# Reordering the opening of a fused Fourier-mixing and SiLU kernel: products summed on TensorE, roundings placed elsewhere, other queues for the last rows

## The chip, the cores and the metric

The kernel runs on one core of a Trainium2 chip. The metric is the device time of one execution in microseconds (us); the time before is 2628.63 us, the median of three runs (2626.27 to 2629.31). The five engines of the core work side by side and wait for each other through semaphores: TensorE (PE, its weight loads are PEld), VectorE (DVE), ScalarE (ACT), GpSimd (POOL) and SyncE (SP). SP, ACT and POOL also issue the DMA transfers; each of them does so in its own program order, so a transfer that has to wait holds up everything behind it on the engine that issues it.

## The reference

Two stages, one after the other. The first is a filter in the frequency domain along the sequence, for 8 batches of 3008 positions and 256 channels; the second is a two-layer network with SiLU on each of the 24064 tokens, with 2048 hidden features.

```python
X = np.fft.rfft(x, axis=1)                    # x: (8, 3008, 256)
F = (filt_r + 1j * filt_i)[None, :, :]        # (1505, 256)
y = np.fft.irfft(X * F, n=x.shape[1], axis=1).astype(np.float32)

t = y.reshape(8 * 3008, 256)
h = t @ w_in                                  # (256, 2048)
g = h * (1.0 / (1.0 + np.exp(-h)))
out = (g @ w_out).astype(np.float32)          # (2048, 256)
```

The weights arrive as float64 words and are made into float32 on the chip (below: a rounding).

## The kernel before

The network runs as a long loop in which TensorE is kept full; the Fourier stage of batch b+1 is spread over the loop that works on batch b. Only batch 0 has nothing to hide behind: its Fourier stage, with the loads and the roundings of the first weights, is the opening, and the loop starts when it is done. The change touches the opening alone. Its stages, in order:

1. Loads of the input, the filter, tables and raw weights. `stage1_first(k)`, k = 0 to 15: two products into one PSUM bank each, then a VectorE transpose out of the bank.
2. For each of six groups g: `forward(g)` (TensorE), `multiply(g, k)` for the two banks k (VectorE: the bank times the real and times the imaginary filter, giving z and p), `add(g, k)` (the complex product from z and p), `inverse_first(g)` (TensorE, then two ScalarE copies and two stores to DRAM).
3. `load_t4(g)` for g = 0 to 3: the stored rows come back, transposed by the addressing. Rows 0 to 39 are those of groups 0 to 4, rows 40 to 47 those of group 5. They are loaded in two parts.
4. `stage3(g)` for g = 0 to 3: TensorE, and a copy of each bank into y by VectorE or ScalarE. With y the loop can begin.

Between these the roundings `rounded(j, ...)` of weights 0 to 8 are run, on VectorE and ScalarE in turn.

```python
def multiply(g, k):
    z = zpool.tile([128, 2, C], FP32, name=f"z_{b}_{g}_{k}", tag="z")      # 4 buffers
    pt = ppool.tile([128, 2, C], FP32, name=f"p_{b}_{g}_{k}", tag="p")     # 2 buffers
    for m, dst in ((0, z), (1, pt)):
        nc.vector.tensor_tensor(out=dst, in0=banks[g][k],
                                in1=f_t[m][:, g, k:k + 1, :].to_broadcast([128, 2, C]), op=ALU.mult)
    prods[g].append((z, pt))

def add(g, k):
    z, pt = prods[g][k]
    eng = nc.vector if b > 0 or (g == NG - 1 and k == 0) else nc.gpsimd
    eng.tensor_tensor(out=z[:, 0], in0=z[:, 0], in1=pt[:, 1], op=ALU.subtract)
    eng.tensor_tensor(out=z[:, 1], in0=z[:, 1], in1=pt[:, 0], op=ALU.add)

def inverse_first(g):
    ps = [bank(b, f"pc_{b}_{g}_{i}") for i in range(2)]
    zs = [z for z, _ in prods.pop(g)]
    for h in range(2):
        table = e_t[:, g] if h == 0 else minus[g // 4][:, g % 4]
        for ri in range(2):
            for i in range(2):
                rows = slice(64 * i, 64 * i + 64)
                for k in range(2):
                    nc.tensor.matmul(out=ps[i][64 * k:64 * k + 64, h, :], lhsT=table[rows, k, ri, :],
                                     rhs=zs[k][rows, ri, :], ...)             # 16 products
    for i, pool, tag in ((0, qpool, "q"), (1, opool, "o")):
        qt = pool.tile([128, 2, C], FP32, name=f"q_{b}_{g}_{i}", tag=tag)
        nc.scalar.copy(out=qt, in_=ps[i])
        a0 = 8 * g + 4 * i
        queue = nc.sync if g == NG - 1 and i == 0 else nc.scalar
        queue.dma_start(out=d2[a0:a0 + 4]..., in_=qt)

def load_t4(g, first=0, last=2 * NS):
    ...                                        # groups 2 and 3 take buffers of the pool "t"
    for h in range(2):
        queue = nc.scalar if first > 0 and h == 1 else nc.sync
        queue.dma_start(out=t4s[g][64 * h + first:64 * h + last],
                        in_=d2[first:last, 4 * g:4 * g + 4, h, :])
```

`bank` gives batch 0 the six PSUM banks in turn, two for each call of `forward`, `inverse_first` and `stage3`. A rounding of two weights is, in order: on VectorE two bit operations for each weight; on ScalarE two activations for each and two more for the even one; on VectorE two multiply-adds, a clamp and two merges; then `place_weights` (two products for each weight) and, behind an odd weight, `combine_weights` (four sums).

The order of the opening:

```python
weights(0, 1)                                  # weights(...): loads of raw words, on SP
place = part["load_first"]()
rounded(0, 1, part=0)
...                                            # loads of filter, tables, weights 2 to 8; table "minus"
for k in range(16):
    part["stage1_first"](k)
rounded(0, 1, part=1)
for g in range(NG):
    part["forward"](g)
    for k in range(2):
        part["multiply"](g, k)
    for k in range(2):
        part["add"](g, k)
    if g > 0:
        part["inverse_first"](g - 1)
    if g in (1, 3):
        rounded(g + 1, g + 2)
for g in range(4):
    part["load_t4"](g, 0, 40)
part["inverse_first"](NG - 1)
for g in range(4):
    part["load_t4"](g, 40, 2 * NS)
for u in range(2):
    second["load_x"](u)
rounded(6, 7)
rounded(8)
for g in range(4):
    part["stage3"](g)
weights(9, 10, 11, 12, 13)
```

Of the kernel before, what the change touches and what calls it, by code (L numbers as in the profile page):

```python
# [46 lines left out]
FP32 = mybir.dt.float32  # L47
U32 = mybir.dt.uint32
AFT = mybir.ActivationFunctionType
# [4 lines left out]
B, S, C = 8, 3008, 256  # L54
DFF = 2048
N1, N2 = 47, 64
NS, NG = 24, 6
# [110 lines left out]
def kernel(  # L168
# [9 lines left out]
    nc = tc.nc  # L178
# [14 lines left out]
    cpool = pool("consts", 1)  # L193
# [4 lines left out]
    tpool = pool("t12", 2)  # L198
    ppool = pool("p", 2)
# [4 lines left out]
    abcpool = pool("abc", 2)  # L204
# [14 lines left out]

    w_t = cpool.tile([128, NJP, 7, 2, 128], FP32)  # L220
    warm = cpool.tile([128, 1], FP32)
    bias_t = cpool.tile([128, 4], FP32)
    x_all = xpool.tile([128, 2, 2, 2 * C], FP32)
    x_t = [x_all[:, i] for i in range(2)]

# [37 lines left out]
    def spectral(b):  # L263
# [171 lines left out]

        def multiply(g, k):
            z = zpool.tile([128, 2, C], FP32, name=f"z_{b}_{g}_{k}", tag="z")
            pt = ppool.tile([128, 2, C], FP32, name=f"p_{b}_{g}_{k}", tag="p")
            for m, dst in ((0, z), (1, pt)):
                nc.vector.tensor_tensor(  # L440
                    out=dst, in0=banks[g][k],
                    in1=f_t[m][:, g, k:k + 1, :].to_broadcast([128, 2, C]), op=ALU.mult)
            prods[g].append((z, pt))

        def add(g, k):
            z, pt = prods[g][k]
            eng = nc.vector if b > 0 or (g == NG - 1 and k == 0) else nc.gpsimd
            eng.tensor_tensor(out=z[:, 0], in0=z[:, 0], in1=pt[:, 1], op=ALU.subtract)
            eng.tensor_tensor(out=z[:, 1], in0=z[:, 1], in1=pt[:, 0], op=ALU.add)

# [13 lines left out]
                                             skip_group_check=True)  # L464
            halves[g] = ps, []

        def inverse_first(g):

            ps = [bank(b, f"pc_{b}_{g}_{i}") for i in range(2)]
            zs = [z for z, _ in prods.pop(g)]  # L470
            for h in range(2):
                table = e_t[:, g] if h == 0 else minus[g // 4][:, g % 4]
                for ri in range(2):
                    for i in range(2):
                        rows = slice(64 * i, 64 * i + 64)
                        for k in range(2):

                            nc.tensor.matmul(out=ps[i][64 * k:64 * k + 64, h, :], lhsT=table[rows, k, ri, :],  # L478
                                             rhs=zs[k][rows, ri, :], start=(h == 0 and ri == 0),
                                             stop=(ri == 1), skip_group_check=True)  # L480
            for i, pool, tag in ((0, qpool, "q"), (1, opool, "o")):
                qt = pool.tile([128, 2, C], FP32, name=f"q_{b}_{g}_{i}", tag=tag)
                nc.scalar.copy(out=qt, in_=ps[i])
                a0 = 8 * g + 4 * i
                queue = nc.sync if g == NG - 1 and i == 0 else nc.scalar
                queue.dma_start(out=d2[a0:a0 + 4].rearrange("a n h c -> (a n) h c"), in_=qt)

        def even(g, i, n=1):
            qt = qpool.tile([128, 2, 2, C], FP32, name=f"q_{b}_{g}_{i}", tag="q")
# [14 lines left out]
        def load_t4(g, first=0, last=2 * NS):  # L504
            if first == 0 and b == 0 and g in (2, 3):
                t4s[g] = tpool.tile([128, 4, C], FP32, name=f"t4_{b}_{g}", tag="t")
            elif first == 0:
                t4s[g] = t4pool.tile([128, 4, C], FP32, name=f"t4_{b}_{g}", tag="t4")
            for h in range(2):
                queue = nc.scalar if first > 0 and h == 1 else nc.sync  # L510
                queue.dma_start(out=t4s[g][64 * h + first:64 * h + last],
                                in_=d2[first:last, 4 * g:4 * g + 4, h, :])

# [302 lines left out]
    def place_weights(j):  # L816
        mf, ef = raws.pop(j)
        for w in range(2):
            cols = slice(256 * w, 256 * w + 256)
            dst = places(j, w) if w == 0 else places(j, w).rearrange("p k (q i) -> p k q i", q=4)  # L820
            v.tensor_tensor(out=dst, in0=columns(mf[:, cols], w), in1=columns(ef[:, cols], w),
                            op=ALU.mult)
        if j % 2 and not 8 < j < 15:
            combine_weights(j // 2)

    def load_exact(j):
        for k in range(2):
            nc.sync.dma_start(out=places(j, 0)[:, k],
                              in_=moe_w_in[128 * k:128 * k + 128, 128 * j:128 * j + 128])
            nc.sync.dma_start(out=places(j, 1)[:, k].rearrange("p (q i) -> p q i", q=4),  # L830
                              in_=columns(moe_w_out[128 * j:128 * j + 128, :], 1)[:, k])
        if j % 2 and not 8 < j < 15:
            combine_weights(j // 2)

    def combine_weights(jp, part=None):

        def w(c):
            return w_t[:, jp, c]
        if part != 1:
            combine(v, w(S1), w(S3), w(A22), ALU.add)  # L840
            combine(v, w(S2), w(S1), w(A11), ALU.subtract)
        if part != 0:
            combine(v, w(S3), w(A11), w(S3), ALU.subtract)
            combine(v, w(S4), w(A12), w(S2), ALU.subtract)

    def weights(*js):
        for j in js:
            if wide:
                load_weights(j)

    def rounded(*js, part=None):

        if wide and part != 1:
            round_weights(*js)
        for j in js:
            if wide and part != 0:
                place_weights(j)
            if not wide and part != 0:
                load_exact(j)
# [4 lines left out]
    for i, value in enumerate((-896.0, 255.0, 255.0 * (1 << 23))):  # L864
        nc.gpsimd.memset(bias_t[:, i:i + 1], value)
    for j in range(4):
        nc.gpsimd.memset(bias_t[32 * j:32 * j + 32, 3:4], 1.0 if j % 2 == 0 else -1.0)
    part, second = spectral(0), spectral(1)
    weights(0, 1)
    place = part["load_first"]()  # L870
# [9 lines left out]
    weights(*range(4, 9))  # L880

    minus = [typool.tile([128, 4, 2, 2, 64], FP32, name=f"minus_{i}", tag="ty") for i in range(2)]
    for g in range(NG):
        nc.scalar.activation(out=minus[g // 4][:, g % 4], in_=e_t[:, g], func=AFT.Identity,
                             scale=bias_t[:, 3:4])
    for k in range(16):
        part["stage1_first"](k)
    rounded(0, 1, part=1)
    for g in range(NG):
        part["forward"](g)  # L890
        for k in range(2):
            part["multiply"](g, k)
        for k in range(2):
            part["add"](g, k)
        if g > 0:
            part["inverse_first"](g - 1)
        if g in (1, 3):
            rounded(g + 1, g + 2)
    for g in range(4):
        part["load_t4"](g, 0, 40)  # L900
    part["inverse_first"](NG - 1)
    for g in range(4):
        part["load_t4"](g, 40, 2 * NS)
    for u in range(2):
        second["load_x"](u)
    rounded(6, 7)
    rounded(8)
    for g in range(4):
        part["stage3"](g)
    weights(9, 10, 11, 12, 13)  # L910
    early[0] = None
    plan_rest(0, part)
    for g in (4, 5):
# [77 lines left out]
```

## Time and profile before

The span of the profiled execution is 2626.4 us. The times below are from its start; "records" are instructions as the profiler counts them, and a float32 product leaves two.

| stage | from, us | to, us |
|---|---|---|
| first product of `stage1_first` to last transpose | 14.73 | 35.36 |
| first `multiply` (group 0) to last `multiply` (group 5) | 38.11 | 76.95 |
| last product of `inverse_first(5)` | | 80.83 |
| first store of group 5 issued, last one issued | 82.26 | 86.35 |
| last rows of `load_t4` issued | 92.82 | 94.44 |
| `stage3`, four groups | 94.91 | 109.31 |
| first product of the loop | 110.27 | |

The page's first part gives the busy time of each engine over the whole span, its second part the busy tenths in 40 slices; the first two slices are the opening. A row of the timeline has the start, the duration, the engine, the line of the kernel, the operation with its tiles, and in brackets how long the engine was idle before it and what it had waited for. A row of the table by stretches has the length, then for each engine the busy time and the number of records, and at its end the TensorE clock (1.00 is full), the busy share of the DMA engines and what they moved.

### The profile page before, as it was taken

Reading aid. Unit: us, or ns where it says so; the run is one execution under the profiler, and the core shown is the slowest. Engines: PE = TensorE matmul, PEld = TensorE weight load, DVE = VectorE, ACT = ScalarE, POOL = GpSimd, SP = SyncE. Lnnn points to the kernel's source line nnn. Section 1 sums busy time; section 2 is a strip of 40 time slices with the busy share of each in tenths; the row PEclk is TensorE's granted clock in tenths of the full one; section 3 lists DMA queues with packets and bytes.
Section 4 is the critical chain, followed back from the end, with each engine's and each line's share of the span. In section 5 each row is a group of like instructions: output and inputs, shape, how many; then the busy total and the mean of one; then the engine's idle time right before and its main releaser. Section 6 shows DMA issues by size and latency. Waiting matters only on the chain.

```text
span 2626.4 us, 47875 instructions
## 1 busy us (share of the span) xinstructions
PE 2554.7 (97%) x18688; PEld 2173.0 (83%) x18688; DVE 1706.6 (65%) x3590; ACT 1104.3 (42%) x3015; POOL 424.3 (16%) x662
## 2 busy tenths in 40 slices
PE   5599999999999999999999999999999999999998
PEld 3378888888888888888888888888888888888987
DVE  6676766666666666666666666666766666555554
ACT  2354444444444444444444434444344444444443
POOL 1121112111211111111112111221112111100100
PEclk8699999999999999999999999999999999999999
DMA  7432222312332123222222322232122311210000
GB/s 234 140 96 61 65 57 72 85 45 64 79 71 65 45 73 71 63 65 72 66 57 56 81 66 62 63 76 62 65 63 69 82 45 29 56 22 21 9 17 16
DMA packets 200267, 171.05 MB, mean 65 GB/s; under 512 B 122212, under 2 KB 174276, under 8 KB 199252
## 3 DMA queue, kind: packets, MB, share of 16 engines
q1 hardware_dynamic: 178808, 117.46, 18.4%
q0 software_dynamic: 16704, 44.06, 5.4%
q10 hardware_dynamic: 4528, 6.46, 0.8%
q8 instruction: 147, 2.41, 0.4%
q14 instruction: 80, 0.66, 0.1%
HBM read 96.05 MB, written 81.26 MB: 68 GB/s over the span
## 4 chain that ended last, share of the span: by engine, by line
PE 95%; DMA 2%; DVE 1%; ACT 1%; ACTq 0%; POOL 0%; issue 0%; SPq 0%; DVEq 0%; POOLq 0%
PE acc L693 43%; PE px L634 26%; PE pyz L634 19%; PE pd L523 3%; PE pb L428 2%; PE pc L461 2%; PE pf L398 1%; PE pa L326 1%; PE pa L335 0%; DMA w_t<-in_x_dram 0%; PE pc L478 0%; DMA d<-q 0%; DMA filt<-in_filt_r_dram 0%; DMA t<-d 0%; DMA d_t<-d_tbl 0%; DVE w_t L605 0%
## 5 line engine op out<-in xcount | busy, mean ns | idle before, releaser
L693 PE MATMUL acc<-g,w_t 128*128 128x256 f32 (+1 forms) x5376 | 1512.0, 375 | 0.4 <-DVE g L605 0.4
L693 PEld LDWEIGHTS acc<-g,w_t 128*128 128x128 f32 x5376 | 1021.3, 190 | 115.7 <-DVE g L605 0.8
L605 DVE TENSOR_TENSOR g<-pyz,abc 128x256 f32<-128x256 f32 (+1 forms) x1152 | 479.9, 417 | 539.8 <-ACT abc L655 298.6
L605 DVE TENSOR_TENSOR g<-g 128x256 f32<-128x256 f32 (+3 forms) x1152 | 616.9, 535 | 196.8 <-ACT g L638 183.6
L634 PE MATMUL px<-ty,w_t 128*128 128x256 f32 (+1 forms) x2304 | 686.9, 380 | 0.5 <-ACT abc L655 0.5
L638 ACT ACTIVATE g<-g 128x256 f32<-128x256 f32 (+1 forms) x1152 | 472.9, 410 | 245.7 <-DVE g L605 245.7
L605 POOL TENSOR_TENSOR s<-s 128x256 f32<-128x256 f32 (+1 forms) x329 | 259.7, 806 | 1455.0 <-DVE s L711 1404.8
L634 PEld LDWEIGHTS px<-ty,w_t 128*128 128x128 f32 x2304 | 424.0, 190 | 83.3 <-issue 25.3
L634 PE MATMUL pyz<-y,w_t 128*128 128x256 f32 (+1 forms) x1536 | 453.7, 377 | 0.7 <-DVE g L605 0.6
L634 PEld LDWEIGHTS pyz<-y,w_t 128*128 128x128 f32 x1536 | 283.4, 189 | 46.6 <-DVE g L605 5.9
L649 ACT COPY abc<-px 128x256 f32<-128x256 f32 (+1 forms) x384 | 141.5, 368 | 364.4 <-PE px L634 364.4
L638 ACT ACTIVATE g<-px 128x256 f32<-128x256 f32 (+1 forms) x384 | 146.1, 380 | 307.4 <-PE px L634 307.3
L655 ACT COPY abc<-px 128x256 f32<-128x256 f32 (+1 forms) x384 | 144.0, 375 | 309.7 <-PE px L634 309.7
L634 PE MATMUL px<-y,w_t 128*128 128x256 f32 (+1 forms) x768 | 229.8, 381 | 1.0 <-ACT y L246 1.0
L634 PE MATMUL pyz<-ty,w_t 128*128 128x256 f32 (+1 forms) x768 | 225.6, 375 | 0.0
L634 PEld LDWEIGHTS px<-y,w_t 128*128 128x128 f32 x768 | 142.1, 189 | 40.0 <-ACT g L638 15.5
L634 PEld LDWEIGHTS pyz<-ty,w_t 128*128 128x128 f32 x768 | 146.0, 190 | 16.9 <-DVE g L605 0.5
L642 ACT COPY abc<-px 128x256 f32<-128x256 f32 (+1 forms) x384 | 135.3, 352 | 2.7 <-PE px L634 1.3
L244 DVE COPY y<-pd 128x376 f32<-128x376 f32 x64 | 51.2, 806 | 98.2 <-PE pd L523 98.2
L523 PEld LDWEIGHTS pd<-wi_t,t 48*64 48x64 f32 x4096 | 68.9, 140 | 40.7 <-issue 33.8
L523 PE MATMUL pd<-wi_t,t 48*64 48x47 f32 x4096 | 76.6, 239 | 20.7 <-DMA t<-d 14.1
L246 ACT COPY y<-pd 128x376 f32<-128x376 f32 x64 | 51.5, 811 | 90.2 <-PE pd L523 90.2
(83 smaller groups left out, 1305.3 us busy)
## 6 DMA issues: line engine op xcount, KB each, us to landing
t<-d SPq DMA_DIRECT2D x120, 192.0 KB
t<-d SPq DMA_DIRECT2D x84, 256.0 KB
d<-q POOLq DMA_DIRECT2D x84, 256.0 KB, 2.7
out_dram<-o SPq DMA_DIRECT2D x636, 32.0 KB
d<-tf POOLq DMA_DIRECT2D x144, 96.0 KB, 2.4
xr<-in_x_dram SPq DMA_DIRECT2D x6, 1472.0 KB
x_all<-in_x_dram SPq DMA_DIRECT2D x72, 96.0 KB
x_all<-xr SPq DMA_DIRECT2D x72, 96.0 KB
```

The lines of the kernel that those rows point to most:

```text
L244: nc.vector.tensor_copy(out=dst, in_=src)
L246: nc.scalar.copy(out=dst, in_=src)
L428: nc.tensor.matmul(out=ps[k][32 * j:32 * j + 32, ri, :], lhsT=d_t[rows, 4 * g + at, ri, :], rhs=t2[rows, at, :], start=True, stop=True)
L461: nc.tensor.matmul(out=ps[j][64 * k:64 * k + 64, a, :], lhsT=e_t[rows, g + a, k, ri, :], rhs=zs[k][rows, ri, :], start=(a == 0 and ri == 0 ...
L523: nc.tensor.matmul(out=ps[h][c0:c0 + 64, cb, i, :], lhsT=t4s[g][rows, i, 128 * cb + c0:128 * cb + c0 + 64], rhs=wi_t[rows, :], start=True, ...
L605: eng.tensor_tensor(out=out, in0=in0, in1=in1, op=op)
L634: nc.tensor.matmul(out=out, lhsT=w_t[:, jp, c, 0], rhs=rhs, start=start, stop=True, skip_group_check=True)
L638: nc.scalar.activation(out=g[:, k, 0:n], in_=g[:, k, 0:n] if src is None else src, func=AFT.Silu)
L642: nc.scalar.copy(out=sums[:, 0, 0:n], in_=xo)
L649: nc.scalar.copy(out=sums[:, 1, 0:n], in_=xo)
L655: nc.scalar.copy(out=sums[:, 2, 0:n], in_=xo)
L693: nc.tensor.matmul(out=acc[pair][i][:, h, 0:n], lhsT=w_t[:, jp, c, 1], rhs=g[:, k, 0:n], start=(jp == 0 and h == 0), stop=last, skip_group ...
```

## The change

It has five parts, all ahead of the loop.

- **Products summed in the inverse.** For groups 1, 4 and 5 no `add` is run. `inverse_first` takes z and p as they are and adds up four terms in PSUM in place of two: 32 products in place of 16. For the signs it needs two tables, `neg`, made by ScalarE once and kept in the two buffers of the pool "t". One half of the p tiles moves to the pool "abc", so that four are there at a time. The adds of groups 0, 2 and 3 stay on GpSimd.
- **Roundings ahead of the copies.** Weights 2 and 3 are rounded behind `multiply(1)` as before, but stand ahead of the ScalarE copies of group 0; weights 4 and 5 behind `multiply(4)` in place of `multiply(3)`; weights 6 and 7 ahead of `inverse_first(5)` in place of behind the last `load_t4`. The combination of weights 0 and 1 goes behind `multiply(0)`.
- **Other queues.** The half of t4's last rows that ScalarE issued is issued by GpSimd; the store of group 5 that SP issued is issued by ScalarE.
- **Early loads.** The two first loads of batch 1 (`load_x`) and the raw weights 9 to 12 are issued in the middle of the groups, weight 13 behind the roundings.
- **Idle products.** 22 products of the table wx with itself, 128 columns each, whose result nobody reads, run on TensorE from the arrival of that table on, ahead of `stage1_first`.

```diff
@@ multiply, add
-            pt = ppool.tile([128, 2, C], FP32, name=f"p_{b}_{g}_{k}", tag="p")
+            if b == 0 and k == 1:
+                pt = abcpool.tile([128, 3, C], FP32, name=f"p_{b}_{g}_{k}", tag="abc")[:, 0:2]
+            else:
+                pt = ppool.tile([128, 2, C], FP32, name=f"p_{b}_{g}_{k}", tag="p")
-            eng = nc.vector if b > 0 or (g == NG - 1 and k == 0) else nc.gpsimd
+            eng = nc.vector if b > 0 else nc.gpsimd
@@ inverse_first
-        def inverse_first(g):
+        def inverse_first(g, added):
-            zs = [z for z, _ in prods.pop(g)]
+            pairs = prods.pop(g)
                 table = e_t[:, g] if h == 0 else minus[g // 4][:, g % 4]
-                for ri in range(2):
+                terms = [(table[:, :, 0], 0, 0), (table[:, :, 1], 0, 1)]
+                if not added:
+                    terms += [(table[:, :, 1], 1, 0), (neg[h][:, g], 1, 1)]
+                for t, (lhs, which, ri) in enumerate(terms):
...
-                queue = nc.sync if g == NG - 1 and i == 0 else nc.scalar
-                queue.dma_start(out=d2[a0:a0 + 4]..., in_=qt)
+                nc.scalar.dma_start(out=d2[a0:a0 + 4]..., in_=qt)
@@ load_t4
-                queue = nc.scalar if first > 0 and h == 1 else nc.sync
+                queue = nc.gpsimd if first > 0 and h == 1 else nc.sync
@@ place_weights, load_exact
-        if j % 2 and not 8 < j < 15:
+        if j % 2 and j != 1 and not 8 < j < 15:
@@ the opening
+    ps = xps.tile([128, 512], FP32, name="idle", tag="x")
+    for _ in range(22):
+        nc.tensor.matmul(out=ps[:, 0:128], lhsT=wx_t, rhs=wx_t, start=True, stop=True)
...
-    for g in range(NG):
-        nc.scalar.activation(out=minus[g // 4][:, g % 4], in_=e_t[:, g], ...)
+    for i, g, n in ((0, 0, 4), (1, 4, 2)):
+        nc.scalar.activation(out=minus[i][:, 0:n], in_=e_t[:, g:g + n], ...)
+    neg = []
+    for i, scale in enumerate((-1.0, bias_t[:, 4:5])):
+        t = tpool.tile([128, 4, C], FP32, name=f"neg_{i}", tag="t").rearrange("p a c -> p (a c)")
+        neg.append(t[:, 0:128 * NG].rearrange("p (g k n) -> p g k n", g=NG, k=2))
+        nc.scalar.activation(out=neg[i], in_=e_t[:, :, :, 0], func=AFT.Identity, scale=scale)
     for k in range(16):
         part["stage1_first"](k)
+    for u in range(2):
+        second["load_x"](u)
     rounded(0, 1, part=1)
+    by_tensor = (1, 4, 5)
     for g in range(NG):
         part["forward"](g)
         for k in range(2):
             part["multiply"](g, k)
-        for k in range(2):
-            part["add"](g, k)
+        if g == 0:
+            combine_weights(0)
+        if g not in by_tensor:
+            for k in range(2):
+                part["add"](g, k)
+        if g in (1, 4):
+            rounded(*((2, 3) if g == 1 else (4, 5)))
+            weights(*((9, 10) if g == 1 else (11, 12)))
         if g > 0:
-            part["inverse_first"](g - 1)
-        if g in (1, 3):
-            rounded(g + 1, g + 2)
+            part["inverse_first"](g - 1, g - 1 not in by_tensor)
     for g in range(4):
         part["load_t4"](g, 0, 40)
-    part["inverse_first"](NG - 1)
+    rounded(6, 7)
+    part["inverse_first"](NG - 1, False)
     for g in range(4):
         part["load_t4"](g, 40, 2 * NS)
-    for u in range(2):
-        second["load_x"](u)
-    rounded(6, 7)
     rounded(8)
+    weights(13)
     for g in range(4):
         part["stage3"](g)
-    weights(9, 10, 11, 12, 13)
```

## The prediction

> **What bounds the kernel now.** I read the page first, then the busy time by stretches, then the chain of waits around the end of the opening, then the timeline of VectorE. The page says that TensorE is busy nearly all the time; the table by stretches says where it is not.
>
> ```profile
> span 2626.4 us, 47875 instructions
> PE 2554.7 (97%) x18688; PEld 2173.0 (83%) x18688; DVE 1706.6 (65%) x3590; ACT 1104.3 (42%) x3015; POOL 424.3 (16%) x662
> ```
>
> ```profile
> 15.00:38.00 23.00, 20.00 (x128) 12.72 (x127) 17.35 (x24) 2.50 (x6) 0.00 (x0) 1.00 0.92 245
> 38.00:80.00 42.00, 22.03 (x311) 11.93 (x315) 35.81 (x65) 12.47 (x21) 16.18 (x22) 0.72 0.35 121
> 80.00:94.90 14.90, 0.82 (x14) 0.36 (x7) 0.02 (x1) 2.07 (x4) 0.00 (x0) 0.69 0.52 168
> 94.90:110.20 15.30, 7.74 (x256) 7.39 (x256) 11.91 (x24) 7.32 (x12) 0.00 (x0) 0.50 0.76 233
> 125.00:200.00 75.00, 74.38 (x433) 58.38 (x432) 53.18 (x124) 37.51 (x97) 19.50 (x35) 1.00 0.40 106
> ```
>
> The reader is to see that the loop leaves TensorE idle for 0.6 of 75 us, while up to 110.2 it is busy for about half the time. What the opening loses or saves is therefore carried to the end, and nothing else in the change can count. The opening has three bounds in turn: VectorE from 35 to 77 us (35.81 busy of 42), then nobody from 80 to 94.9, when transfers are waited for, then VectorE again.
>
> ```profile
> 80.74 2.04 DMA d<-q
> ...
> 82.97 2.99 DMA t<-d
> ...
> 86.35 6.45 DMA d<-q
> ...
> 92.82 0.60 ACTq L511
> ...
> 94.49 0.72 ACT scratch L797
> ...
> 97.96 1.31 DVE scratch L812 x2
> ...
> 106.50 0.71 DVE y L244
> ...
> 107.25 2.10 PE pd L523 x62
> ...
> 110.27 1.19 PE px L634 x2
> ```
>
> This is the end of the opening in the chain of waits. One store of group 5 stands on SP behind eight loads of t4, goes out at 86.35 and takes 6.45 us among them. ScalarE then holds its own loads of t4 until 92.82, so the roundings behind them start at 94.49 only, and the copies into y stand behind the roundings on VectorE (106.50). The fourth `stage3` needs the banks that those copies free.
>
> **What the skill says.** The Trainium skill, "TensorE: Matmul & The Clock Gate", section "Part 1: The HAM clock gate", has TensorE at half clock until it has been busy for about 3.4 us, in a window that runs free, and at half clock again after such a window idle. The trace agrees in kind: pairs of products in `stage1_first` start 1.71 us apart (18.14, 19.85, 21.56) and from 24.54 on 0.87 us apart, so 9 us went by at half speed; the clock at 94.90 to 110.20 is 0.50 after 14 us idle. Its section "Part 3: Packing small matmuls" lets products on different quarters of the array run together: the inverse (64 by 64) shows it, 16 products from 45.98 to 47.87 together with their minus half, about 0.11 us each at full clock, and some 0.21 at half (3.4 us for a set from 41.69). "GPSIMD Engine Reference", section "1. Specifications", has GpSimd share its SBUF interfaces with VectorE. The trace agrees: rounding operations take 0.41 to 0.44 us (79.28), but 0.94 to 1.01 beside the adds. "DMA: Bandwidth & Descriptors", Specifications, gives a GpSimd-issued transfer 0.4 us more to the first byte than one of SP or ACT. Here GpSimd's land in 2.7 us by the page, ACT's short ones in about 2.
>
> ```profile
> 42.96 1.01 DVE L795 TENSOR_SCALAR scratch<-raw 128x512 uint32<-128x512 uint32 x1
> ...
> 48.30 0.73 DVE L807 SCALAR_TENSOR_TENSOR scratch<-raw,scratch 128x512 f32<-128x512 uint32 x1 [2.23 <-ACT scratch L799]
> ...
> 54.77 0.68 DVE L440 TENSOR_TENSOR z<-pb,filt 128x512 f32<-128x512 f32 x1
> ...
> 95.76 0.69 DVE L807 SCALAR_TENSOR_TENSOR scratch<-raw,scratch 128x512 f32<-128x512 uint32 x1 [15.74 <-ACT scratch L799]
> ```
>
> In these VectorE rows the first pair's rounding runs from 42.96 to 54.77, 11.8 us, with a wait of 2.23 for ScalarE, which is at its copies. The last pair waited 15.74.
>
> **The change part by part.** I count from T, the end of the transposes (35.36 us before).
>
> *Idle products.* 22 products of 128 columns run at 0.43 us cold (the 128-column pairs of `stage1_first` show that spacing), 9.5 us if all cold and less if the clock comes. wx lands at some 3 us, so they end between 10 and 12.7, and x lands at 14.6: a gap of 2 to 4.6 us. If the clock survives it, the first four pairs run at 0.87 in place of 1.71 us and T falls by 4 times 0.83, about 3.3 us, for VectorE needs 0.88 a transpose anyway. If not, T stays. I take one half: 1.6 us gained.
>
> *Up to group 3.* Placing weights 0 and 1 takes 1.3, two groups of `multiply` 2.4 each, the four sums 1.5; these sums now lie beside the adds of group 0, and about two run slow, so 1.1 more. Rounding 2 and 3 starts at T + 8.7 (7.6 before). Without adds beside it, and with ScalarE free, it should take what the pair 6 and 7 shows from ScalarE's start at 94.49 to 102.2, plus 0.4: 8.2 us. Groups 2 and 3 then run from T + 16.9 to T + 21.7; group 2 began at T + 19.4 before. Gain so far 2.5 us.
>
> *Group 4.* It comes at once where a rounding stood. Its bank is filled behind `inverse_first(2)`, which needs the GpSimd adds of group 2: four of 0.7 us from T + 18.2, ended T + 21.1, the inverse 3 us behind that as before (58.97 to 61.88), `forward` 1.1: VectorE can begin group 4 at T + 25.3, idle for 3.6 us, and ends it at T + 27.7. Rounding 4 and 5, 8.2 us, ends at T + 35.9, group 5 at T + 38.3. Before, group 5 ended at 76.95, T + 41.6. Gain 3.3 us; it would be 7 without the new wait.
>
> *Summing.* Group 5 loses its adds, which on two engines took 1.8 us past the last `multiply` (76.95 to 78.7), but has 32 products: 3.4 us at full clock, 6.9 at half. They can start 0.6 before the last `multiply` ends. Between `inverse_first(4)`, ended about T + 33.5, and this one lie 4 us idle, so I expect something between: end at T + 43.2. Before: 80.83, T + 45.5. Summing takes back about 1 of the 3.3 us.
>
> *Stores and last rows.* ScalarE copies at once (0.6 each) and issues both stores by +1.4 us; rounding 6 and 7 of ScalarE (3.7 us from T + 38.7) is out of its way by then. But the loads of t4 for groups 2 and 3 go into the buffers of the two `neg` tables, so they can't start until `inverse_first(5)` has read them: 640 KB beside 512 KB of stores. At the 200 GB/s that 80.7 to 92.8 shows (some 1.57 MB in 10 us, less 2 of latency) that is 5.8 us; both stores landed at +6.5, taken with a little luck. The last rows add 0.1 and 2.1 on SP, 2.7 and half a microsecond of issue on GpSimd: +9.2, so `stage3` begins at T + 52.4. Before it was 94.91, T + 59.6: 14.1 us behind the inverse, 9.2 now. Gain 4.9.
>
> *Roundings and copies.* Weights 6, 7 and 8 end on VectorE at T + 38.3 + 8.2 + 4.3 = T + 50.8, before `stage3`. So the copies follow the products, and the 6.67 us for which the fourth group waited go. Four groups at the 1.9 us that 192 records in 5.68 show are 7.6; the last copy and the start of the loop 1.0, as before (109.31 to 110.27). First product of the loop at T + 61.0, before 110.27 = T + 74.9.
>
> *Early loads.* They were not on the path before; they now lie where the DMA share was 0.35. Nothing gained, except that SP is free. Weights 11 and 12 (1 MB) go out when rounding 4 and 5 has read its words, about T + 33, beside stores of groups 3 and 4: part of the risk below.
>
> The sum: 74.9 - 61.0 = 13.9, plus 1.6 for T, gives 15.5 us. I add 1 for what I counted pessimistically (`inverse_first(5)` cold, the stores among the loads) and predict 2628.6 - 16.6 = 2612 us.
>
> **The rivals.**
> - *The transfers take the place of the wait removed.* For it: t4 of groups 2 and 3 behind `neg`, and weights 11 and 12 in the same stretch. If the stores need 6.45 us again behind ACT's issue and first rows of groups 0 and 1 are late too, `stage3` starts 4 to 5 us later and the gain is 11: 2617. Against: the store of group 5 no longer stands behind eight loads on SP.
> - *TensorE becomes the bound.* `stage3` and the last inverse are cold, 6.9 and 7.6 us, and the summing adds 16 products for each of three groups. Groups 1 and 4 hide under roundings (8.2 us); group 5 doesn't. All cold costs 2 us more; all warm gives 3 to 5 us: 2607.
> - *The idle products do it all or nothing.* The whole 3.3 us kept gives 2610; if they delay the input's first products, nothing: 2614. The first gap before inverse work (37.4 to 41.7, nearly idle) ended with a cold array, which speaks against.
> - *The gain is lost in the loop*, to a wait on batch 1's loads or on weights 9 to 15. The same stretch is 74.38 of 75 busy now and those loads come earlier, so I give this 5 in 100.
>
> **Range and chances.** Gains from 10 (transfers collide, clock lost) to 23 us (clock kept, warm inverse, quiet transfers): 2605 to 2619 holds 8 in 10. 2% are 53 us, half the opening, so within 2% has 0.985, faster 0.01, slower 0.005.
>
> **What would show it.** Transposes starting 0.88 us apart from the first on: clock kept. The VectorE wait ahead of group 4's first `multiply` near 3.6 us: the new bound. The rounding of 2 and 3 near 8.2 us. The time from the last inverse product to the first of `stage3` near 9 in place of 14.1 us. No wait in `stage3`, and the first product of the loop near 93 to 95. If that comes at 93 and the time doesn't fall by as much, the loop lost it; if it comes above 100, the transfers or group 4 are worse than I think.

## The result, and the profile after

The changed kernel takes 2616.82 us, the median of four runs (2616.4 to 2618.97). Against the kernel before (2628.35 us in four runs beside it) the ratio is 0.9959, with a 95% interval of 0.9942 to 0.9976. That is 11.5 us less, where the prediction had 16.6.

The first part of the page of the changed kernel:

```profile
span 2615.2 us, 48142 instructions
PE 2568.0 (98%) x18828; PEld 2186.7 (84%) x18828; DVE 1703.3 (65%) x3588; ACT 1104.4 (42%) x3013; POOL 419.4 (16%) x660
```

TensorE is busy for 13 us more in a span that is 11 us shorter: the idle products alone are 7.99 us, and the summing adds 48 products. The chain of waits of the changed kernel from the last inverse on (start, duration, what):

```profile
81.06 6.16 DMA d<-q
87.30 2.45 DMA t<-d
89.84 0.42 PE pd L529 x2
90.26 1.49 issue
91.75 3.87 PE pd L529 x135
95.62 0.57 issue
96.19 3.51 PE pd L529 x119
...
100.61 1.19 PE px L640 x2
```

The first product of the loop comes at 100.61 in place of 110.27, so the opening gave 9.7 us. The chain no longer passes through roundings or through a copy into y by VectorE: the 6.67 us wait inside `stage3` is gone, as foreseen. What stands there now is a store of 6.16 us and two breaks in `stage3` (1.49 and 0.57), in which PE waits for nothing that the chain names: rows of t4 are still missing, as the experiments show. VectorE's rows in the changed kernel:

```profile
43.91 0.41 DVE L801 TENSOR_SCALAR scratch<-raw 128x512 uint32<-128x512 uint32 x1
...
52.10 0.68 DVE L443 TENSOR_TENSOR z<-pb,filt 128x512 f32<-128x512 f32 x1
...
61.24 0.69 DVE L443 TENSOR_TENSOR z<-pb,filt 128x512 f32<-128x512 f32 x1 [4.19 <-PE pb L428]
```

Weights 2 and 3 are rounded from 43.91 to 52.10, 8.2 us in place of 11.8. The rounding operation is 0.41 us in place of 1.01, as no add runs on GpSimd beside it. Group 4 then waits 4.19 us for its bank; group 5 ends at 74.3. Two rows of the table by stretches of the changed kernel:

```profile
72.60:79.50 6.90, 6.74 (x64) 3.50 (x64) 6.09 (x13) 3.75 (x7) 0.00 (x0) 0.62 0.61 208
89.80:99.80 10.00, 7.74 (x256) 7.32 (x256) 2.52 (x4) 2.50 (x4) 0.49 (x1) 0.50 0.31 66
```

`stage3` is as cold as before, at a clock of 0.50. The inverse of group 5 is colder than before: it stood directly behind that of group 4, and from 79.00 to 80.83 the clock was 1.00; now TensorE is idle for 5.01 us ahead of it, and the clock is 0.62.

The spans of the two profiled executions differ by 11.2 us, so 1.5 us of it are in the loop: span less first product is 2516.1 us before and 2514.6 after. Half of that is the clock, which came sooner: the first four records of `pa` in the loop stand in the chain with 2.13 us in place of 2.85. Over all kernels below, this rest lies between 2513.7 and 2515.9.

### The profile page after: what moved, and what is told of

The parts are those of the page before. It is cut to its first block, busy times and chain, and to the rows that moved or that the text cites. A ratio compares the mean times of both kernels' runs of the same rounds, so it can differ in the third digit from the quotient of the medians.

```text
span 2615.2 us, 48142 instructions
## 1 busy us (share of the span) xinstructions
PE 2568.0 (98%) x18828; PEld 2186.7 (84%) x18828; DVE 1703.3 (65%) x3588; ACT 1104.4 (42%) x3013; POOL 419.4 (16%) x660
## 4 chain that ended last, share of the span: by engine, by line
PE 96%; DVE 1%; DMA 1%; ACT 0%; issue 0%; POOL 0%; DVEq 0%; SPq 0%; ACTq 0%; POOLq 0%
PE acc L699 43%; PE px L640 26%; PE pyz L640 19%; PE pd L529 3%; PE pb L428 2%; PE pc L464 2%; PE pf L398 1%; DMA x_all<-in_x_dram 1%; PE pa L326 0%; PE pa L335 0%; DVE w_t L295 0%; PE pc L485 0%; DMA t<-d 0%; DMA d<-q 0%; DMA raw<-in_moe_w_in_dram 0%
## 5 line engine op out<-in xcount | busy, mean ns | idle before, releaser
L640 PEld LDWEIGHTS px<-y,w_t 128*128 128x128 f32 x768 | 142.3, 190 | 39.8 <-ACT g L644 15.5
L529 PE MATMUL pd<-wi_t,t 48*64 48x47 f32 x4096 | 76.6, 239 | 12.5 <-DMA t<-d 10.4
```

The source lines that it names most:

```text
L529: nc.tensor.matmul(out=ps[h][c0:c0 + 64, cb, i, :], lhsT=t4s[g][rows, i, 128 * cb + c0:128 * cb + c0 + 64], rhs=wi_t[rows, :], start=True, ...
L640: nc.tensor.matmul(out=out, lhsT=w_t[:, jp, c, 0], rhs=rhs, start=start, stop=True, skip_group_check=True)
```

## The experiments

The edits below start from the changed kernel, but for two that start from the kernel before. T is again the end of the transposes. Three landmarks are compared: `stage3`'s first product, the first product of the loop (px), and the median. Of the changed kernel they are 89.84, 100.61 and 2616.82. Where an edit does not touch T it still lies anywhere from 35.2 to 36.8, as the input arrives. Each kernel has one profiled execution, and even counted from T, px differs by 1.7 us between the changed kernel and the one without idle products (65.46 and 63.77), which are alike behind T. Smaller differences of px are not read as effects by themselves.

### Idle products left out

```diff
-    for _ in range(22):
-        nc.tensor.matmul(out=ps[:, 0:128], lhsT=wx_t, rhs=wx_t, start=True, stop=True)
```

> The changed kernel without its 22 idle products. Theory A (the clock they raise is lost again in the 3.25 us gap before the input lands and in the 2.26 us gap behind the first product, so they bought nothing): last transpose ends within 0.6 us of the changed kernel's 35.1 us, first product of the loop within 1 us of 100.6, time within 1.5 us of 2616.8. Theory B (they bring part of the gain, as one half of 3.3 us in the prediction): last transpose 1.5 to 3.3 us later, time 2618.5 to 2620.

Measured: 2616.02 us (2615.26 to 2617.4), ratio 0.9956 [0.994, 0.9973] (in brackets the 95% interval, here and below); T 35.45, px 99.22. The idle products brought nothing. TensorE's timeline of the changed kernel shows why:

```profile
3.65 7.99 PE L878 MATMUL idle<-wx_t 96*128 96x128 f32 x44 [3.65 <-DMA wx_t<-wx_tbl]
14.89 0.88 PE L293 MATMUL pa<-w_t,wx_t 96*128 96x384 f32 x2 [3.25 <-DMA w_t<-in_x_dram]
18.03 0.79 PE L293 MATMUL pa<-x_all,wx_t 96*128 96x128 f32 x2 [2.26 <-DMA x_all<-in_x_dram]
18.61 1.49 PE L293 MATMUL pa<-w_t,wx_t 96*128 96x384 f32 x2
...
23.49 0.81 PE L293 MATMUL pa<-w_t,wx_t 96*128 96x384 f32 x2
```

The first large product behind them takes 0.88 us, so it ran at full clock: the clock survived the gap of 3.25 us. The 128-column product after the second gap, of 2.26 us, takes 0.79 in place of 0.39, and the large ones behind it 1.49 in place of the 0.81 that comes at 23.49. The clock was lost between 15.8 and 18, while the second half of the input was waited for. The prediction saw the first gap and not the second. (The clock column of the tables reads 1.00 from 15 to 38 us in the kernel before, although the products there are slow; it is the spacing of the products that shows the half clock.)

### Products up to the input and across its gap

```diff
-    for _ in range(22):
+    for _ in range(38):
@@ stage1_first: the 384-column product of bank k+3 goes ahead of the 128-column product of bank k
+            for j in range(k + 3 if k else 0, min(k + 4, 16)):
+                us[j] = bank(b, f"pa_{b}_{j}")...
+                product(j, 0, 0, 24)
+            product(k, 1, 24, 8)
```

> The changed kernel with 38 idle products, which should reach to the landing of the input at 14.8 us, and with the 384-column products of four banks ahead of the first 128-column one, so that TensorE has work while the last part of the input is waited for. Theory A (the idle products failed for their gaps alone): transposes 0.88 us apart from the first on, last one ends near 32.8 in place of 35.1, and as VectorE sets the pace behind it, the first product of the loop comes 1.5 to 2.3 us earlier, time near 2614.8. Rival (the loads set the pace there, or the raw weights 2 and 3 aren't there in time): transposes end early, but the rounding of weights 2 and 3 waits for its words, and less than 0.7 us is left at the first product of the loop.

Measured: 2614.06 us (2613.6 to 2616.53), 0.995 [0.9936, 0.9965]; T 33.24, px 97.13. TensorE's timeline of this kernel:

```profile
9.64 5.98 PE L883 MATMUL idle<-wx_t 96*128 96x128 f32 x50
15.46 2.75 PE L292 MATMUL pa<-w_t,wx_t 96*128 96x384 f32 x8
18.41 0.49 PE L292 MATMUL pa<-x_all,wx_t 96*128 96x128 f32 x2 [0.21 <-DMA x_all<-in_x_dram]
18.74 0.81 PE L292 MATMUL pa<-w_t,wx_t 96*128 96x384 f32 x2
```

With four large products in the second gap, that gap is 0.21 us, and from then on everything runs at full clock. T falls by 1.9 us: three cold pairs were left to save, at 0.84 each, and the input came 0.4 us later (18.41 against 18.03). px comes 2.1 us earlier than without idle products, as much as T does, so what T gains is carried on. The idea of the idle products was right; they ended too early, and nothing filled the wait for the second half of the input.

### Group 5 added again

```diff
-    by_tensor = (1, 4, 5)
+    by_tensor = (1, 4)
-    part["inverse_first"](NG - 1, False)
+    part["inverse_first"](NG - 1, True)
```

Its adds are shared by VectorE and GpSimd, as before the change. This frees the `neg` tables one inverse earlier; by the prediction, t4's loads for groups 2 and 3 wait for them.

> The changed kernel with group 5 added as before the change (k 0 on VectorE, k 1 on GpSimd) and 16 products in its last inverse in place of 32; groups 1 and 4 stay summed. Theory A (the summing of group 5 runs at half clock, 6.7 us, and holds the neg tables that the loads of t4 for groups 2 and 3 wait for): the last inverse product ends 0.5 to 1.5 us earlier than 79.4, the loads of groups 2 and 3 start when the fourth group's inverse is done and not at the fifth's, the last store lands 2 to 4 us earlier than 87.2, first product of the loop 2.5 to 5 us earlier, time 2612 to 2614.5. Rival B (the summing helps group 5 as intended): last inverse later, first product of the loop 0 to 2 us later. Rival C (the stores are slow for another reason): the inverse ends earlier but the store still takes about 6 us.

Measured: 2616.48 us (2615.81 to 2617.15), 0.9958 [0.9943, 0.9973]; `stage3` 90.94, px 101.10. Nothing moved by more than the noise. The stores of group 5 still need 5 us (83.39 to 88.37), and the first load of t4 goes out at 78.61, against 76.64 (T + 42.0 and 41.5). So it was not `neg` that held this first load. In the changed kernel the last store of group 4 is issued at 71.48 and lands near 76.6, and the first load of t4 follows it at once: the stores are slow, beside the raw loads of weights 11 and 12 issued from 68.90 on.

### The last rows by ScalarE again, with its rounding out of the way

```diff
     part["inverse_first"](NG - 1, False)
+    rounded(8)
     for g in range(4):
         part["load_t4"](g, 40, 2 * NS)
-    rounded(8)
@@ load_t4
-                queue = nc.gpsimd if first > 0 and h == 1 else nc.sync
+                queue = nc.scalar if first > 0 and h == 1 else nc.sync
```

> The changed kernel with the half of t4's last rows that GpSimd issues given back to ScalarE, and the rounding of weight 8 ahead of these loads so that it is not held up behind them. Theory A (GpSimd's issue and later landing cause the two breaks of 1.49 and 0.57 us in stage3): stage3 runs without a break, 7.7 to 8.2 us in place of 9.9, first product of the loop 1.5 to 2.5 us earlier, time 2614.5 to 2615.5. Rival B (the breaks come from the landing of many short transfers, whoever issues them): stage3 still takes 9.5 us or more, time unchanged within 1 us.

Measured: 2612.35 us (2610.83 to 2613.65), 0.9942 [0.9927, 0.9957]; `stage3` 88.41, px 97.51. It is the largest gain of the edits to the changed kernel up to here, 4.5 us. First GpSimd's part in the changed kernel: the timeline of its issues, and the line of the DMA view of 66 to 94 us (operation, count, size of one, median us from issue to landing):

```profile
87.91 2.38 POOL L517 DMA_DIRECT2D t<-d  x4 [28.84 <-DMA d<-q]
```

```profile
t<-d POOLq DMA_DIRECT2D x4, 32.0 KB, 4.5
```

GpSimd needs 2.38 us to issue four loads of 32 KB, and the median one lands 4.5 us after its issue. Then TensorE's timeline of the experiment:

```profile
88.41 2.44 PE L529 MATMUL pd<-wi_t,t 48*64 48x47 f32 x64 [7.77 <-DMA t<-d]
91.25 5.29 PE L529 MATMUL pd<-wi_t,t 48*64 48x47 f32 x192 [0.41 <-DMA t<-d]
97.51 0.67 PE L640 MATMUL px<-y,w_t 128*128 128x256 f32 x2 [0.97 <-ACT y L246]
```

`stage3` is 8.1 us long with a break of 0.41, in place of 9.9 with 2.06. Counted from T, px falls by 4.1 us: 1.8 of it in `stage3`, the rest ahead of it, where the rows behind the stores of group 5 could go out 4.1 us after the last store's issue in place of 6.16. The edit does not change those stores, and why they were quicker was not found. In part it is chance in the changed kernel's one profiled execution: its second break of 0.57 is missing in the kernels without idle products, with the longer stretch and with group 5 added, whose first breaks are 1.59 to 1.71 and whose px lies at 63.8 to 64.5 from T. Against these the edit gains 2.4 to 3.1 us at px (61.4), and `stage3` is 1.0 to 1.1 us shorter. The loop also starts at full clock here (px in 0.67 in place of 1.19 us).

### Weights 11 and 12 loaded behind the roundings

```diff
-            weights(*((9, 10) if g == 1 else (11, 12)))
+            if g == 1:
+                weights(9, 10)
@@
-    weights(13)
+    weights(11, 12, 13)
```

> The changed kernel with the loads of raw weights 11 and 12 (1 MB) moved from behind multiply(4) to behind the last loads of t4. Theory A (they collide with the stores of groups 3 and 4, which land some 5 us after their issue and so hold up the first loads of t4 until 76.6 us): the first load of t4 goes out 2 to 3 us earlier, the loads of groups 0 and 1 are through before the stores of group 5, these land in 4 to 5 us in place of 6.2, first product of the loop 1 to 2.5 us earlier. Rival B (the loads of groups 2 and 3, held by the neg tables until the last inverse, are what slows the stores of group 5): first load of t4 earlier, but these stores still take 5.5 us or more, and the loop starts within 0.7 us of the changed kernel's.

The next kernel does this too, and also keeps `neg` in spare words of two buffers of raw weights, so that the pool "t" is free for t4 from the start:

```diff
-        t = tpool.tile([128, 4, C], FP32, name=f"neg_{i}", tag="t")...
-        neg.append(t[:, 0:128 * NG]...)
+        neg.append(raws["spare", 2 * i]...)
```

> As the run before, and the two neg tables lie in spare words of the raw weights' buffers in place of the buffers of t4's groups 2 and 3, so that no load of t4 waits for the last inverse. Theory B (the neg tables hold up half of t4's loads and these the stores of group 5): all eight loads go out in one row near 74 us, are landed near 81, the stores of group 5 land in 2 to 3.5 us in place of 6.2, stage3 starts 2.5 to 4 us earlier than with 11 and 12 moved alone, first product of the loop near 96 to 97.5 us, time 2612 to 2614. Theory A alone: no further gain over the run before.

Measured: 2619.02 us (2616.88 to 2619.45), 0.9958 [0.9942, 0.9975], px 103.37 without, and 2617.4 (2616.84 to 2618.04), 0.9955 [0.994, 0.997], px 100.12 with `neg` moved. Neither gained. The chain of waits of the second:

```profile
81.31 2.64 DMA d<-q
...
84.04 2.15 DMA t<-d
...
86.44 0.41 PE pd L529 x2
86.85 1.60 issue
88.45 3.87 PE pd L529 x135
92.32 3.38 issue
95.70 3.51 PE pd L529 x119
```

The cause was right. With 11 and 12 moved, the last store of group 4 lands within 2.1 us (issued at 73.28, first load of t4 at 75.35) in place of 5.2, and the stores of group 5 need 3.62 us in place of 6.16; `neg` moved as well takes that to 2.64, and `stage3` starts at 86.44 in place of 89.84. So the raw loads are the larger part of the delay, and `neg` about a microsecond. But all of it is given back inside `stage3`. The raw loads are now issued by SP directly behind its rows, and GpSimd's rows land among them: the breaks are 1.60 and 3.38 us in place of 1.49 and 0.57 (2.13 and 3.23 without `neg` moved). The bulk load was moved from beside the stores to beside the rows, and the slower queue paid.

### The queues alone, and weights 6 and 7 alone, on the kernel before

```diff
-                queue = nc.sync if g == NG - 1 and i == 0 else nc.scalar
-                queue.dma_start(out=d2[a0:a0 + 4]..., in_=qt)
+                nc.scalar.dma_start(out=d2[a0:a0 + 4]..., in_=qt)
@@
-                queue = nc.scalar if first > 0 and h == 1 else nc.sync
+                queue = nc.gpsimd if first > 0 and h == 1 else nc.sync
```

> The kernel before with the queues of the change alone: group 5's store on ScalarE, the half of t4's last rows on GpSimd. Theory A (the queues are the larger part of the gain, as ScalarE is no longer held for 12 us and the store no longer stands behind eight loads): stage3 starts near 91 to 92 us in place of 94.9, roundings end near 95.5 in place of 106.4, first product of the loop near 101 to 102 us in place of 110.3: 8 to 9 us of the 9.7 that the whole change gained there; time 2619 to 2620.5. Rival (the order of the groups and the summing carry half): 104 us or later, time 2623 or more.

```diff
+    rounded(6, 7)
     part["inverse_first"](NG - 1)
...
-    rounded(6, 7)
     rounded(8)
```

> The kernel before with the rounding of weights 6 and 7 moved ahead of the last inverse, nothing else. Theory A (it takes out the wait for the copies into y, but not the one for the rows): stage3 starts near 95 as before, the fourth group waits 1 us or less in place of 6.7, first product of the loop near 103 to 104.5, gain 6 to 7 us, time near 2622; added to the run of the queues alone this is more than the whole change gained, as both take out the same wait. Rival (ScalarE's rounding ahead of its copies of group 5 puts the stores off by its 3.7 us, and the rows with them): stage3 starts 3 us later and the gain is 3 to 4 us, time near 2625.

Measured: the queues alone 2622.46 us (2620.31 to 2624.86), 0.9977 [0.9969, 0.9986]; the rounding alone 2621.87 (2620.78 to 2622.91), 0.9972 [0.9961, 0.9983]. The chain of waits with the queues alone, and then with the rounding alone:

```profile
88.69 6.92 DMA t<-d
95.61 4.36 PE pd L522 x149
99.97 0.56 issue
100.53 3.24 PE pd L522 x107
```

```profile
86.87 6.87 DMA d<-q
93.75 2.10 DMA t<-d
...
95.99 7.30 PE pd L523 x256
```

In both `stage3` starts no earlier than before (95.6 and 96.0 against 94.91), and in both the 6.67 us wait within it is gone. The rounding alone does what was expected of it. The queues alone fall short: GpSimd issues its rows from 87.57 on, 5 us earlier than ScalarE did, but the median one takes 7.5 us to land, so `stage3` waits as long as before. px comes at 104.62 and 104.20, 5.7 and 6.1 us earlier. Together that would be 11.7, more than the 9.7 of the whole change: the two take out the same wait, for the roundings of weights 6 and 7 that stood behind ScalarE's own loads. Either suffices for it. Counted from T, px is at 67.98 and 68.61, at 65.46 in the whole change, and at 74.91 before. So at px the whole change is 2.5 us ahead of the queues alone and 3.2 ahead of the rounding alone; by the medians it is 5.6 and 5.1 us, of which a part is a later T (36.64 and 35.59) and a longer rest of the loop in these two. That is what all the rest is worth, together with what the two do jointly beyond either. The two without the rest were not run.

### Weights 4 and 5 behind group 3 again

```diff
-        if g in (1, 4):
+        if g in (1, 3):
```

> The changed kernel with the rounding of weights 4 and 5 (and the loads of 11 and 12) back behind multiply(3). It takes away what makes group 4 wait for 4.2 us on VectorE. Theory A (that wait can't be had: the inverses of groups 4 and 5 then stand back to back on a cold TensorE): the wait is gone and the last multiply ends 1 to 2.5 us earlier after the last transpose, but the last inverse product and the first product of the loop come within 1 us of the changed kernel's. Rival B (the wait is lost time): last inverse 2 us earlier or more, first product of the loop 1.5 to 3 us earlier, time 2614 to 2615.5.

Measured: 2617.58 us (2617.45 to 2620.01), 0.9961 [0.9948, 0.9975]; px 100.42. Group 4's wait of 4.19 us is gone and group 5 ends 2.4 us earlier, at 71.8, yet the loop starts at the same time, as theory A has it. The rows of VectorE show where the time went:

```profile
72.79 0.42 DVE L804 TENSOR_SCALAR scratch<-raw 128x512 uint32<-128x512 uint32 x1
77.51 0.69 DVE L813 SCALAR_TENSOR_TENSOR scratch<-raw,scratch 128x512 f32<-128x512 uint32 x1 [4.29 <-ACT scratch L805]
```

VectorE waits 4.29 us for ScalarE, which waits until 74.20 for `inverse_first(4)`, now cold and 5.76 us long; then come its copies of group 4, then its half of the rounding of 6 and 7, and only then the copies of group 5. Its last store is issued at 81.51, against 81.06. The wait moved from one engine to another.

### No summing at all

```diff
-    by_tensor = (1, 4, 5)
+    by_tensor = ()
-    part["inverse_first"](NG - 1, False)
+    part["inverse_first"](NG - 1, True)
```

> The changed kernel with no group summed on TensorE: groups 1 and 4 added on GpSimd, group 5 on VectorE and GpSimd as before the change; 16 products in every inverse. Everything else of the change stays. Theory A (summing is worth what the adds do to VectorE beside them): the first rounding operations of weights 2 and 3 and of 4 and 5 take 0.9 to 1.0 us again in place of 0.42, some 1.9 us a pair, the last multiply ends 3 to 4 us later after the last transpose, the last inverse product 2 to 3 us later, first product of the loop near 103, time 2618.5 to 2620. Rival B (the 16 more products for each group cost what the adds did): first product of the loop and time within 1 us of the changed kernel's.

Measured: 2617.18 us (2616.6 to 2618.85), 0.9958 [0.9943, 0.9974]; px 101.48. VectorE's rows of this kernel:

```profile
44.79 0.95 DVE L804 TENSOR_SCALAR scratch<-raw 128x512 uint32<-128x512 uint32 x1
...
62.03 0.69 DVE L443 TENSOR_TENSOR z<-pb,filt 128x512 f32<-128x512 f32 x1 [3.91 <-issue]
```

The rounding operations beside the adds are slow again (0.95 in place of 0.41), but only two or three of each pair. Weights 2 and 3 take 9.0 us (44.21 to 53.25), where the changed kernel has 8.2 and the kernel before 11.8: most of that gain came from the order and not from the summing. The wait ahead of group 4 is still there (3.91) and takes up what the first pair loses. Group 5 ends 1.4 us later counted from T, px comes 0.9 later, and the time is not different. No gain shows from the summing, the largest part of the edit; one of a microsecond or so would not show among executions of one kernel that lie 2.3 to 2.6 us apart.

### What helped, joined

The longer stretch of products, the rows by ScalarE, and the kernel with the late loads and `neg` moved, in one:

> What the runs so far point to, joined: the changed kernel with 38 idle products and the four first 384-column products ahead, neg in spare words of the raw weights' buffers, weights 11 and 12 behind t4's last rows, these rows' second half on ScalarE behind the rounding of weight 8. Theory (the four terms that were mis-sized are separate: clock 2.3 us, loads behind neg and beside weights 11 and 12 about 3.5, GpSimd's rows 2 and more): last transpose near 33, last inverse product near 77.5, both stores landed near 82, stage3 from about 84 without a break over 0.5 us, first product of the loop 92 to 94 us in place of 100.6, time 2608 to 2611. Rival (they share one wait, as the two halves of the change did against the kernel before): first product of the loop later than 96, time 2612 or more.

Measured: 2612.41 us, 0.9938 [0.9926, 0.995]; `stage3` 83.76, 8.1 us long without a break, px 92.86. The landmark came 7.75 us earlier than in the changed kernel, as the theory has it, the median only 4.4, which is in the rival's range and no better than ScalarE's rows alone (2612.35). The profiled execution took 2609.46 us, the four others 2611.99 to 2613.31. Why the others are longer stays open; that the four terms add up is therefore shown for one execution only.

Then 20 idle products ahead of the last inverse and 30 behind it:

```diff
+    idle(20)
     part["inverse_first"](NG - 1, False)
+    idle(30)
     rounded(8)
```

> The joined kernel with idle products in the two gaps that are left on TensorE: 20 between the inverses of groups 4 and 5, 30 behind the latter. Theory (the half clock is the term that is left: the last inverse takes 6.7 us for what 3.4 would do, stage3 7 to 8 for some 5, and the loop's first products 1 us in place of 0.5): last inverse about 3.5 us long and ended near 73.7 in place of 76.9, rows landed 2 to 3 us earlier, stage3 then held by the copies into y, which the rounding of weight 8 lets go at 84.3, first product of the loop 88 to 90 us in place of 92.9 and at full clock, time 3 to 6 us under the joined kernel's 2612.4. Rival (the clock is not held by products of 128 columns across these gaps, or the stores take as much longer beside the loads as they start earlier): first product of the loop within 1 us of 92.9, time 2611 to 2613.

Measured: 2609.33 us (2606.92 to 2610.01), 0.9926 [0.9913, 0.994], the best of all; its interval overlaps that of the run above. TensorE's timeline of it:

```profile
64.74 4.73 PE L885 MATMUL idle<-wx_t 96*128 96x128 f32 x40
69.83 0.61 PE L490 MATMUL pc<-z,e_t 64*64 64x256 f32 x2 [0.35 <-DVE z L448]
...
74.53 6.96 PE L885 MATMUL idle<-wx_t 96*128 96x128 f32 x60
82.91 3.26 PE L534 MATMUL pd<-wi_t,t 48*64 48x47 f32 x133 [1.41 <-DMA t<-d]
87.42 3.65 PE L534 MATMUL pd<-wi_t,t 48*64 48x47 f32 x123 [1.26 <-issue]
91.95 1.22 PE L645 MATMUL px<-y,w_t 128*128 128x256 f32 x2 [0.88 <-ACT y L246]
```

The last inverse runs at full clock from 69.83 to 74.5, 4.7 us in place of 6.7; 3.5 were hoped for. But the stores, issued at 76.08 and 77.12, have landed by some 80.6 only, and the last rows at 84.2. `stage3`, behind a pause of 1.41 us, runs at a clock of 0.61 and breaks off for 1.26. So px gained 0.9 us of the 3 to 5 that were hoped for, as the rival has it. The median fell by 3.1, more than the landmark explains.

## Why the prediction was right, and where its steps were off

The time fell within the range, near its upper end, by the mechanism named: the roundings of weights 6 and 7 no longer stand behind ScalarE's own loads, and what the opening saves is carried to the end. The point of 2612 was 4.8 us too low: px came at T + 65.5 in place of T + 61.0, and above the 100 us that the text had named as a sign of transfers or group 4 being worse. Step by step, from T:

- *Idle products*: a gain of 1.6 us was put down, 0.2 came. Half a chance was given to the clock's surviving one gap; there were two, and the second took it. The Trainium skill, "TensorE: Matmul & The Clock Gate", section "Part 1: The HAM clock gate", puts the idle window that loses the clock at about 3.4 us; here no gap was that long, and 3.25 and 2.26 us with 0.9 us of work between were enough. So the measurement decides: the longest single gap did not settle it. Kept at full clock, T does fall by 1.9.
- *Groups 2 to 5*: rounding 2 and 3 at T + 8.8 and 8.2 us long (8.7 and 8.2), group 4's wait 4.19 (3.6), group 5's end T + 39.1 (38.3). The step held. That group 4's wait is the new bound, as it said, is true for VectorE only: taken away in one run, it left the loop's start where it was.
- *Summing*: the last inverse ended at T + 44.3 (43.2), cold as feared. The step put its cost at about 1 us for group 5. Undone for group 5 and for all groups, the time did not differ.
- *Stores and last rows*: +9.2 us was predicted, 10.4 came. The sum itself left out the half microsecond of issue: 6.5, 2.7 and 0.5 are 9.7. (Its 200 GB/s is right, but by a wrong working: 1.57 MB is SP's queue alone; with ScalarE's it is 2.36 MB in 12.1 us.) Both stores had landed at +7.8 in place of +6.5. The prediction put the delay down to `neg`; the runs show the raw loads of weights 11 and 12 as the larger part, as they slow the stores of group 4 and so the first loads of t4. They were in the text as a risk without a number of their own.
- *`stage3`*: 7.6 us was predicted, 9.9 came. This is the mis-sized term. GpSimd's share of the rows was counted at 2.7 us and half a microsecond of issue. Measured were 2.38 us to issue four and 4.5 to land, and up to a further 3.4 us of break beside loads of other queues. The figure of 2.7 was the page's median for GpSimd's 256 KB stores, nearly all of them in the loop, not for loads beside other queues. The Trainium skill, "DMA: Bandwidth & Descriptors", Specifications, which the prediction leaned on, has only the first byte 0.4 us later; here the measurement decides. Of the 2.3 us by which `stage3` was too long, 0.57 is the second break, which the kernels like it lack.
- *Roundings and copies*: the wait of 6.67 us went, as said. This was the main gain, and the runs with one part each show that either the queues or the earlier rounding was enough.

The terms add up: 1.4 us for T, 0.8 for the groups, 0.3 for the last inverse, 1.2 for stores and rows, 2.3 for `stage3`, less 0.1 at the loop's start, are the 5.9 us by which the opening's gain fell short of 15.5. The 1 us that was added for pessimism did not come either, as the last inverse was cold and the stores were slow. The loop gave 1.5 us that no step had counted, half of it by the clock.

Of the rivals, the first (transfers take the place of the wait: 2617) came true in kind. That its figure was met is in part luck: it had `stage3` start 4 to 5 us later than predicted, and it started 2.3 later; the rest is the clock at the input (1.4) and the breaks inside `stage3` (2.3). The second holds half: TensorE was cold in both places, but warming the last inverse gained less than a microsecond at px, because transfers then bound. Of the third, the half "nothing" came true. The loss in the loop did not come.

## What to carry to other kernels

When two engines issue transfers in program order, look first for compute that stands behind a waiting issue; here moving either one alone was worth 6 of the 11.5 us of a large edit. A bulk load that nobody needs soon costs where it lies beside short transfers on the chain, and moving it from the stores to the loads moves the wait along with it. Put the short transfers that end a stage on the queues that issue fast (here SP and ScalarE). If work is added to keep TensorE at full clock, it has to reach right up to the data, every gap counted.

## What was not expected of the hardware

- Four loads of 32 KB issued by GpSimd took 2.38 us to issue and 4.5 us each (median) to land, 7.5 in the kernel with the queues alone. The same loads by ScalarE took 1.62 us to issue in the run with its rows back, and `stage3` broke off for 0.41 us in place of 2.06.
- A store of 256 KB to DRAM lands in 2.0 us when little runs beside it (80.74 before) and in 6.2 to 6.9 beside loads (81.06 in the changed kernel, 86.87 with the rounding alone).
- The clock at the loop's first product was full behind 5.29 us of `stage3` without a break in one kernel, and half behind 8.1 us without a break in the joined one (px in 0.67 and 1.19 us). Why was not found.
